# Attention and routed experts on one core: the casts of v move from GpSimd to VectorE and ScalarE

## The chip, the cores and the metric

The kernel runs on one core of a Trainium2 chip. TensorE (PE) multiplies, VectorE (DVE), ScalarE (ACT) and GpSimd (POOL) do elementwise work, and SyncE (SP) only issues transfers. SP, ACT and POOL can each issue DMA transfers, which run on the core's 16 DMA engines. Every engine works through its own queue of instructions strictly in order; an instruction that waits holds up all that stand behind it on that engine. The metric is the device time of one execution in microseconds.

## What is computed

Linear attention, then a mixture of eight experts with weights from a Sinkhorn iteration:

```python
def phi(x): return np.where(x > 0, x, np.exp(x) - 1.0) + 1.0
q_p, k_p = phi(q), phi(k)                  # q, k, v: 8 batches, 8 heads, 576 rows, 64 columns, f32
kv = np.einsum('bhsd,bhse->bhde', k_p, v)
z = np.sum(k_p, axis=2)
num = np.einsum('bhsd,bhde->bhse', q_p, kv)
den = np.einsum('bhsd,bhd->bhs', q_p, z)[..., None] + 1e-06
x = num / den                              # taken as 4608 rows of 512
P = np.exp(x @ w_gate - max)               # then eight rounds: rows and columns of P normalised
for e in range(8):
    out += P[:, e:e+1] * (np.maximum(x @ w1[e], 0.0) @ w2[e])    # w1[e]: 512x1024, w2[e]: 1024x512
```

## The kernel before

**Stages.** The front computes attention in 16 half batches, numbered n = 0 to 15 (batch n // 2, four heads each), in the function `att` (L237). Expert 0 runs beside the front in plain form (`unit_plain`, L695, with its first layer in `layer1`, L520), in nine groups of 512 rows, since its groups need only the finished rows of x. Experts 1 to 7 come after, in a form with seven block products in place of eight (`unit`, L766), whose operands are DVE sums of weight blocks (`combos`, L736). The Sinkhorn iteration (L415) needs the logits of all rows and gives the factors P by which every expert's output is scaled.

**One half batch.** Three inputs of 576 KB each (kin, qin, vin) are loaded (L253). For k and q, ACT takes the exponential (L266, tiles ek and eq, f16); DVE clamps it at 1 (L275) and takes the maximum with x + 1 (L281, two instructions; or ACT adds 1 at L272 and DVE takes one maximum at L278), giving tk and tq. v is cast from f32 to f16 into vv, beside a column of ones (L295 and L225). Two such vv buffers alternate. PE then multiplies tk by vv (kv_ps, L306), transposes tq (qt_ps, L332), forms the denominators (den_ps, L347) and the numerators in three parts (num_ps, L371). DVE takes the reciprocal (rden, L353) and multiplies (xn, L376); PE transposes xn (xt_ps, L387) and ACT or DVE copies it into xT (L221 or L223). The inputs, ek and eq together, tk, tq and most others have two buffers each, so the load for n + 2 waits for the last reader of n.

**Expert 0.** `layer1` computes hq = w1 x in eight tiles of 128 columns for each group, each a sum of four matmuls over the contraction (512 rows in four blocks c of 128; L536), and ACT applies the maximum with 0 (L540, tile h). Blocks 0 and 1 of x come from the even half batch, 2 and 3 from the odd one. hq has two PSUM buffers. The second layer (ye, L706) reads h and w2.

**Weights.** `load_w` (L192) loads and casts w1 and w2 of an expert through DMAs on POOL's queue; each kind has two buffers. For expert 0 both come in two halves. w1 of expert 0 is made to depend on the cast of v of n = 0 (`vcast[0]`, L490), w2 of expert 0 on the inputs of n = 3. Inputs of n = 2 and 3 are issued by POOL too, all others by SP.

**What sets the order.** All work is handed to `_Plan` (L18) with an engine, a duration in microseconds, dependencies and a priority. Its `run` method plays the schedule through with these durations and gives the instructions out in the order that comes of it. `LAT` and `OVER` are its figures for the hand-over between engines. What it emits is fixed: the engines later follow their queues in that order, whatever the real durations. A DMA is a task of 1.55 (an input) on one serial engine, and 2.6 until it can be used. The loads of expert 1's weights carry a start time that only the plan knows:

```python
w_t[1] = load_w1(1, prio=0.0, after=110.0) + load_w2(1, prio=0.0, after=115.0)
```

On the chip such an instruction runs when those ahead of it in POOL's queue have run and its own semaphores have come. In the built order of before, POOL's queue in the front is: v cast of n = 0, w1 of expert 0 (two DMAs), kin and qin of n = 2, v cast of n = 1, vin of n = 2, the three inputs of n = 3, w2 of expert 0 (two DMAs), w_gate, the 14 other casts of v, w1 and w2 of expert 1. 34 matmuls on a tile of zeros (L476) keep PE warm at the start. From expert 1 on, the order of PE's work is written out by hand (L885).

Of the kernel before, what the change touches and what calls it, by code (L numbers as in the profile page):

```python
# [10 lines left out]
FP32 = mybir.dt.float32  # L11
FP16 = mybir.dt.float16
# [5 lines left out]
class _Plan:  # L18
# [14 lines left out]
    def add(self, eng, fn, deps=(), prio=0.0, acq=(), use=(), lat=0.0, after=0.0):  # L33

        if isinstance(eng, tuple):
            eng = {eng[0]: eng[1]}
        k = len(self.t)
        t = {"eng": eng, "fn": fn, "prio": prio, "acq": tuple(acq), "lat": lat, "kids": [], "nd": 0,
             "ready": after, "done": None, "id": k}
        self.t.append(t)  # L40
        for d in set(x for x in deps if x is not None):
            self.t[d]["kids"].append(k)
            t["nd"] += 1
        for g in list(acq) + list(use):
            g["users"].append(k)
        return k
# [76 lines left out]
def kernel(  # L123
# [10 lines left out]
    nc = tc.nc  # L134

    B, H, S, D = q.shape
# [4 lines left out]
    P = 128  # L141
    PW = 64
    NJ = S // PW
    NG = N // 512
    NTT = N // P
    NFT = F // P
    NDT = DM // P
# [3 lines left out]
    S_ = _Plan()  # L151
    add = S_.add

    const = ctx.enter_context(tc.tile_pool(name="const", bufs=1))
# [3 lines left out]
    hqp = ctx.enter_context(tc.tile_pool(name="hqp", bufs=2, space=PSUM))  # L158
# [18 lines left out]
    fp = front.enter_context(tc.tile_pool(name="fp", bufs=2))  # L177
# [1 line left out]
    kvz_t = [fp.tile([P, 2, 2, D + 1], FP16, tag=f"kvz{i}", name=f"kvz{i}", bufs=1) for i in range(2)]  # L179

    p_in = {n: S_.pool(2) for n in "kvq"}
    p_e = S_.pool(2)
    p_t = {n: S_.pool(2) for n in "kq"}
    p_vv, p_kvz, p_qpT, p_xn, p_rden = (S_.pool(2) for _ in range(5))
    p_att, p_hq, p_h = S_.pool(2), S_.pool(2), S_.pool(2)
# [33 lines left out]
    def copy(e, dst, src):  # L219
        if e == "act":  # L220
            nc.scalar.copy(out=dst, in_=src)  # L221
        elif e == "dve":
            nc.vector.tensor_copy(out=dst, in_=src)  # L223
        else:
            nc.gpsimd.tensor_copy(out=dst, in_=src)  # L225
# [4 lines left out]
    vcast = {}  # L230

    def fadd(*a, **kw):
        t = add(*a, **kw)
        front_ids.append(t)
        return t

    def att(b, g):  # L237
        n = 2 * b + g
        pr = n - 100.0
# [7 lines left out]
        gin, tin, gt, tph = {}, {}, {}, {}  # L247
        for nm, ten in (("k", k), ("q", q), ("v", v)):
            gr = gin[nm] = S_.grp(p_in[nm])

            def fn(_, gr=gr, nm=nm, ten=ten):
# [5 lines left out]
                      deps=[w_last[0] if n in (2, 3, 4) else None, in_prev[0]])  # L257
            in_prev[0] = ti
            tin[nm] = fadd(("dma", 1.55), lambda _: None, deps=[ti], use=[gr], prio=pr, lat=2.6)
        for nm in "kq":  # L260
            ge = S_.grp(p_e)
            gt[nm] = S_.grp(p_t[nm])

            def f_e(_, ge=ge, nm=nm):
                ge["tile"] = fp.tile([P, 2, NJ, D], FP16, tag="e", name="e" + nm)
                nc.scalar.activation(out=ge["tile"], in_=gin[nm]["tile"], func=AF.Exp)  # L266

            def f_t(e, g_=gt[nm], nm=nm):
                g_["tile"] = fp.tile([P, NJ, 2, D], FP16, tag="t" + nm, name="t" + nm)
                g_["on"] = e  # L270
                if e == "act":
                    nc.scalar.add(out=g_["tile"].rearrange("p j r d -> p r j d"), in_=gin[nm]["tile"], add=1.0)  # L272

            def f_m(_, ge=ge, g_=gt[nm], nm=nm):
                nc.vector.tensor_scalar(out=ge["tile"], in0=ge["tile"], scalar1=1.0, scalar2=None, op0=ALU.min)  # L275
                o = g_["tile"].rearrange("p j r d -> p r j d")
                if g_["on"] == "act":
                    nc.vector.tensor_tensor(out=o, in0=o, in1=ge["tile"], op=ALU.max)  # L278
                else:
                    for r in range(2):  # L280
                        nc.vector.scalar_tensor_tensor(out=o[:, r], in0=gin[nm]["tile"][:, r], scalar=1.0,  # L281
                                                       in1=ge["tile"][:, r], op0=ALU.add, op1=ALU.max)
            te = fadd(("act", 1.17), f_e, deps=[tin[nm]], acq=[ge], use=[gin[nm]], prio=pr)
            tt_ = fadd({"dve": 0.6, "act": 1.17}, f_t, deps=[tin[nm]],
                       acq=[gt[nm]], use=[gin[nm]], prio=pr)
            tph[nm] = fadd(("dve", 1.35), f_m, deps=[te, tt_], use=[ge, gt[nm], gin[nm]], prio=pr)
        gvv = S_.grp(p_vv)
        tvv = []
# [3 lines left out]
        ta = fadd(("none", 0.0), f_va, deps=[tin["v"]], acq=[gvv], prio=pr)  # L292
        def f_v(e):
            copy(e, gvv["tile"][:, :, :, 0:D], gin["v"]["tile"])
        tvv.append(fadd(("pool", 1.3), f_v, deps=[ta, tin["v"]],  # L295
                        use=[gvv, gin["v"]], prio=pr))
        vcast[n] = tvv[0]
        gkv, gz = [S_.grp(p_ye[2]), S_.grp(p_ye[3])], S_.grp(p_kvz)

        def f_kv(_):  # L300
# [25 lines left out]
        for j0, j1 in ((0, 5), (5, NJ)):  # L326
# [8 lines left out]
            def f_qc(e, j0=j0, j1=j1, gp=gp):  # L335
                copy(e, gq["tile"][:, :, j0:j1, :].rearrange("p h j w -> p j h w"), gp["tile"][:, 0:j1 - j0])
            t1 = fadd(("pe", 0.06 * (j1 - j0)), f_qt, deps=[tph["q"], tqa], acq=[gp], use=[gt["q"]], prio=pr)
            tq.append(fadd({"act": 0.12 + 0.1 * (j1 - j0), "dve": 0.17 + 0.057 * (j1 - j0)}, f_qc, deps=[t1, tqa],
                           use=[gp, gq], prio=pr))
# [23 lines left out]
        for i0, i1 in ((0, 2), (2, 4), (4, 5)):  # L363
# [15 lines left out]
            t1 = fadd(("pe", 0.12 * (i1 - i0)), f_num, deps=[tden, txa], acq=[gn], use=[gq, gz], prio=pr)  # L379
            txn.append(fadd(("dve", 0.14 + 0.275 * (i1 - i0)), f_xn, deps=[t1, trd, txa], use=[gn, grd, gxn], prio=pr))  # L380
        for c2 in range(2):
# [10 lines left out]
            t1 = fadd(("pe", 0.3), f_xt, deps=txn, acq=[gx], use=[gxn], prio=pr)  # L392
# [68 lines left out]
        return add(("dve", 0.8), f_p, deps=last, prio=-200.0)  # L461

    nc.vector.memset(ones_t, 1.0)
    warm = const.tile([P, 512], FP16, tag="warm", name="warm")
    nc.vector.memset(warm, 0.0)

# [18 lines left out]
    for i in range(2):  # L485
        nc.vector.memset(vv_t[i][:, :, :, D], 1.0)
        nc.vector.memset(kvz_t[i], 0.0)
    att(0, 0)
    att(0, 1)
    w_t = {0: load_w1(0, prio=-290.0, parts=2, deps=[vcast[0]])}  # L490
    for b in range(1, B):
        att(b, 0)
        att(b, 1)
        if b == 1:
            w_t[0] += load_w2(0, prio=-96.5, parts=2, deps=[in_prev[0]])
        if b % 2 == 1:
            logits(b // 2)
# [17 lines left out]
    prev_hq = [None]  # L515
# [4 lines left out]
    def layer1(e, g):  # L520
        gw1, tw1, gw2, tw2 = w_t[e]
        bs = range(512 * g // S, (512 * g + 511) // S + 1)
        xd_ = [xt_done[(b, c)] for b in bs for c in range(NDT)]
        th = []
        gh = S_.grp(p_h)

        def f_ha(_):
            gh["tile"] = hpool.tile([P, NFT, 512], FP16, tag="h", name="h")
        tha = add(("none", 0.0), f_ha, deps=[prev_hq[0]], acq=[gh], prio=g - 400.0)
        for f in range(NFT):  # L530
            ghq = S_.grp(p_hq)

            def f_hq(_, f=f, ghq=ghq):
                ghq["tile"] = hqp.tile([P, 512], FP32, tag="hq", name="hq")
                for c in range(NDT):
                    nc.tensor.matmul(ghq["tile"], lhsT=gw1["tile"][:, c, ts(f, P)], rhs=xT[:, c, ds(512 * g, 512)],  # L536
                                     start=(c == 0), stop=(c == NDT - 1))

            def f_rl(_, f=f, ghq=ghq):
                nc.scalar.activation(out=gh["tile"][:, f, :], in_=ghq["tile"], func=AF.Relu)  # L540
            t1 = add(("pe", 0.87), f_hq, deps=[tw1[f // 4], prev_hq[0]] + xd_, acq=[ghq], use=[gw1],
                     prio=g + 0.1 * f + 0.35)
            prev_hq[0] = t1
            x_users.append(t1)
            th.append(add(("act", 0.6), f_rl, deps=[t1, tha], use=[ghq, gh], prio=g - 400.0))
        return gh, [th, th]

# [147 lines left out]
    def unit_plain(e, g, gW=None, tW=None):  # L695
        gw1, tw1, gw2, tw2 = w_t[e]
        gh, th = layer1(e, g) if e == 0 else block7(e, g, gW, tW)
        gy = [S_.grp(p_ye[tt % 2]) for tt in range(4)]
        ty = [None] * 4
# [225 lines left out]
```

The softmax here doesn't subtract the row's maximum and nothing guards it: scores larger than these inputs give would overflow.

## Time and profile before

| | us |
|---|---|
| median of 12 runs (lowest, highest) | 982.49 (981.75, 985.77) |
| the profiled execution | 982.66 |
| its span, from the first to the last instruction | 980.9 |
| PE busy | 961.2 |
| DVE busy | 770.7 |
| ACT busy | 562.9 |
| POOL busy | 128.0 |

The granted TensorE clock was 0.999 on average. The profile shows one execution. The page lists engines with their busy time; the span in 40 slices of equal length, where each digit is a busy share in tenths; and groups of instructions. Besides the page, the trace answers questions: the instructions of a stretch in order of time (start, duration, engine, line, operation, output <- inputs; in brackets, idle time before it and what ended that), sums of waiting by pair of engines (total, times, longest), and tables of busy time by stretch. PE's instructions overlap, so a row of matmuls can be shorter than the sum of their durations.

### The profile page before, as it was taken

To read this page: it belongs to the slowest core of one execution; us is meant where nothing else is said; L and a number is where in the kernel's file an instruction comes from. 1 tells how busy PE (TensorE), PEld (TensorE's weight loads), DVE (VectorE), ACT (ScalarE), POOL (GpSimd) and SP (SyncE) were. 2 spreads that over 40 slices of the span, in tenths; PEclk is the share of its full clock that TensorE was granted. 3 is DMA by queue.
4 is the path that set the end of the run, shared out by engine and by line. 5 is a ranking of instruction groups with operands and counts; after the bars stand their busy time and mean duration, and the time that the engine had idled before them with its cause. 6 is when DMAs were issued, how large, how long until landed. Compare 5 with 4: busy or idle time off the path is not lost.

```text
span 980.9 us, 21403 instructions
## 1 busy us (share of the span) xinstructions
PE 961.2 (98%) x8716; PEld 791.9 (81%) x8716; DVE 770.7 (79%) x1561; ACT 562.9 (57%) x1034; POOL 128.0 (13%) x171
## 2 busy tenths in 40 slices
PE   7899999999999999999999999999999999999997
PEld 3555564488888888888888888888888888888885
DVE  6898869967777777777777777777777777777774
ACT  4898754565555555555555555555555555555552
POOL 5111200001111111111111111111111111111110
PEclk9999999999999999999999999999999999999999
DMA  9987953162226322272226322272225322236663
GB/s 307 289 288 241 277 155 127 66 132 77 74 77 141 95 76 76 76 161 76 75 76 141 96 76 76 77 162 76 76 77 136 102 76 77 76 108 163 161 161 98
DMA packets 47028, 121.99 MB, mean 124 GB/s; under 512 B 4176, under 2 KB 18000, under 8 KB 46928
## 3 DMA queue, kind: packets, MB, share of 16 engines
q1 hardware_dynamic: 32128, 99.76, 30.8%
q0 software_dynamic: 14480, 20.33, 11.6%
q8 instruction: 68, 1.11, 0.4%
q10 hardware_dynamic: 320, 0.52, 0.1%
q14 instruction: 32, 0.26, 0.1%
HBM read 119.69 MB, written 17.69 MB: 140 GB/s over the span
## 4 chain that ended last, share of the span: by engine, by line
PE 89%; DVE 1%; ACT 1%; issue 0%
PE ye L809 33%; PE hq L627 23%; PE att L627 11%; PE Zye L627 6%; PE Zye L809 6%; PE ye L706 5%; PE hq L536 4%; PE xt_ps L387 0%; PE kv_ps L306 0%; PE num_ps L371 0%; PE lg_ps L405 0%; DVE tk L281 0%; PE qt_ps L332 0%; ACT tq L272 0%; PE den_ps L347 0%; ACT qpT L221 0%
## 5 line engine op out<-in xcount | busy, mean ns | idle before, releaser
L823 DVE SCALAR_TENSOR_TENSOR acc<-ye,P_sb,acc 128x256 f32<-128x256 f32 x620 | 264.9, 477 | 95.2 <-PE ye L809 77.8
L627 PEld LDWEIGHTS <-W 128*128 128x128 f16 x2016 | 197.0, 98 | 23.9
L809 PEld LDWEIGHTS <-S 128*128 128x128 f16 x1984 | 194.2, 98 | 22.7 <-issue 0.3
L809 PE MATMUL ye<-T,S 128*128 128x256 f16 x1488 | 192.8, 273 | 0.1
L833 POOL TENSOR_TENSOR acc<-acc,st 128x256 f32<-128x256 f32 x124 | 87.4, 725 | 625.6 <-ACT st L830 620.8
L653 ACT ACTIVATE h<-hq 128x512 f16<-128x512 f32 x126 | 76.5, 607 | 160.9 <-PE hq L627 160.9
L627 PEld LDWEIGHTS <-w 128*128 128x128 f16 x1512 | 147.5, 98 | 23.3 <-issue 1.0
L809 PEld LDWEIGHTS <-h 128*128 128x128 f16 x1488 | 145.6, 98 | 16.8
L627 PE MATMUL hq<-xs,W 128*128 128x256 f16 x1008 | 151.2, 273 | 0.0
L627 PE MATMUL att<-xs,W 128*128 128x256 f16 x1008 | 151.1, 272 | 0.0
L627 PE MATMUL hq<-xs,w 128*128 128x256 f16 x1008 | 140.7, 272 | 0.8 <-DVE h L656 0.8
L782 DVE TENSOR_TENSOR S<-h 128x1024 f16<-128x1024 f16 x124 | 85.4, 688 | 57.9 <-ACT h L653 57.9
L656 DVE CUSTOM_DVE_ANT_0 h<-att,s 128x512 f16<-128x512 f32 x126 | 86.7, 688 | 13.1 <-ACT s L643 13.1
L830 ACT ACTIVATE st<-Zye,P_sb 128x256 f32<-128x256 f32 x124 | 52.0, 470 | 78.0 <-PE Zye L809 78.0
L643 ACT COPY s<-hq 128x512 f32<-128x512 f32 x126 | 75.1, 596 | 36.8 <-PE hq L627 36.8
L650 ACT ACTIVATE h<-Zye 128x512 f16<-128x512 f32 x126 | 75.2, 597 | 35.1 <-PE Zye L627 35.1
L656 DVE CUSTOM_DVE_ANT_0 h<-hq,s 128x512 f16<-128x512 f32 x126 | 86.4, 686 | 0.8 <-PE hq L627 0.7
L639 ACT COPY Zye<-hq 128x512 f32<-128x512 f32 x126 | 73.3, 581 | 16.3 <-PE hq L627 16.3
L706 PE MATMUL ye<-w,h 128*128 128x512 f16 x320 | 77.6, 379 | 0.0
L627 PE MATMUL Zye<-xs,w 128*128 128x256 f16 x504 | 75.6, 273 | 0.0
L647 ACT COPY s<-att 128x512 f32<-128x512 f32 x126 | 74.5, 591 | 0.0
L536 PE MATMUL hq<-xT,w 128*128 128x512 f16 x288 | 70.6, 379 | 2.0 <-ACT h L540 1.7
(90 smaller groups left out, 960.3 us busy)
## 6 DMA issues: line engine op xcount, KB each, us to landing
xs<-xd SPq DMA_DIRECT2D x63, 896.0 KB, 4.6
w<-in_moe_w_dram POOLq DMA_DIRECT2D x14, 1024.0 KB, 11.3
out_dram<-acc SPq DMA_DIRECT2D x68, 128.0 KB, 2.4
kin<-in_k_dram SPq DMA_DIRECT2D x14, 576.0 KB, 6.1
qin<-in_q_dram SPq DMA_DIRECT2D x14, 576.0 KB, 5.5
vin<-in_v_dram SPq DMA_DIRECT2D x14, 576.0 KB, 6.6
xd<-xst SPq DMA_DIRECT2D x9, 512.0 KB, 2.6
xd<-xT SPq DMA_DIRECT2D x9, 256.0 KB, 5.0
```

Source lines behind the costliest of these rows:

```text
L536: nc.tensor.matmul(ghq["tile"], lhsT=gw1["tile"][:, c, ts(f, P)], rhs=xT[:, c, ds(512 * g, 512)], start=(c == 0), stop=(c == NDT - 1))
L627: nc.tensor.matmul(dst[:, p, :], lhsT=lhs(p, c), rhs=rhs(c), start=(first and p == 0 and c == 0), stop=(c == 1), skip_group_check=True)
L643: nc.scalar.copy(out=gs2["tile"], in_=gX["tile"])
L647: nc.scalar.copy(out=gs5["tile"], in_=gR["tile"])
L650: nc.scalar.activation(out=hd(0, 0), in_=Zt[1], func=AF.Relu)
L653: nc.scalar.activation(out=hd(1, 0), in_=gX["tile"], func=AF.Relu)
L656: nc.vector._custom_dve(TENSOR_ADD_SAT, out=dst, in0=ps, in1=sb, s0=3.0e38, s1=0.0)
L706: nc.tensor.matmul(gy[tt]["tile"], lhsT=gh["tile"][:, f, ds(P * tt, P)], rhs=gw2["tile"][:, f, :], start=(f == 0), stop=(f == NFT - 1))
L782: nc.vector.tensor_tensor(out=Sx[:, i], in0=a0, in1=a1, op=op)
L809: nc.tensor.matmul(bank(g_)[:, s, :], lhsT=lhs(s, kk), rhs=rhs(kk), start=(new and s == 0 and kk == 0), stop=(kk == 3), skip_group_check=True)
L823: nc.vector.scalar_tensor_tensor(out=dst(), in0=bank(g_)[:, s, :], scalar=P_sb[:, gg, e:e + 1], in1=dst(), op0=ALU.mult, op1=ALU.add)
L833: nc.gpsimd.tensor_tensor(out=dst(), in0=dst(), in1=gst["tile"], op=ALU.add)
```

## The change

v is cast by ACT for n = 0 and 1 and by DVE for n = 2 to 15. POOL copies four columns of v of n = 0 into a small tile `gate`, and w1 of expert 0 depends on that copy. ek and eq share three buffers, not two. In the first group of expert 0, the first two tiles of hq are computed in halves of the contraction: each product over blocks 0 and 1 is a step of its own that needs only the even half batch.

```diff
--- before.py
+++ after.py
@@ -179,7 +179,7 @@
     kvz_t = [fp.tile([P, 2, 2, D + 1], FP16, tag=f"kvz{i}", name=f"kvz{i}", bufs=1) for i in range(2)]
 
     p_in = {n: S_.pool(2) for n in "kvq"}
-    p_e = S_.pool(2)
+    p_e = S_.pool(3)
     p_t = {n: S_.pool(2) for n in "kq"}
     p_vv, p_kvz, p_qpT, p_xn, p_rden = (S_.pool(2) for _ in range(5))
     p_att, p_hq, p_h = S_.pool(2), S_.pool(2), S_.pool(2)
@@ -262,7 +262,7 @@
             gt[nm] = S_.grp(p_t[nm])
 
             def f_e(_, ge=ge, nm=nm):
-                ge["tile"] = fp.tile([P, 2, NJ, D], FP16, tag="e", name="e" + nm)
+                ge["tile"] = fp.tile([P, 2, NJ, D], FP16, tag="e", name="e" + nm, bufs=3)
                 nc.scalar.activation(out=ge["tile"], in_=gin[nm]["tile"], func=AF.Exp)
 
             def f_t(e, g_=gt[nm], nm=nm):
@@ -292,9 +292,12 @@
         ta = fadd(("none", 0.0), f_va, deps=[tin["v"]], acq=[gvv], prio=pr)
         def f_v(e):
             copy(e, gvv["tile"][:, :, :, 0:D], gin["v"]["tile"])
-        tvv.append(fadd(("pool", 1.3), f_v, deps=[ta, tin["v"]],
+        tvv.append(fadd(("act", 1.17) if n < 2 else ("dve", 0.75), f_v, deps=[ta, tin["v"]],
                         use=[gvv, gin["v"]], prio=pr))
-        vcast[n] = tvv[0]
+        if n == 0:
+            def f_gate(_):
+                nc.gpsimd.tensor_copy(out=gate, in_=gin["v"]["tile"][:, 0, 0, 0:4])
+            vcast[0] = add(("pool", 0.15), f_gate, deps=[tin["v"]], use=[gin["v"]], prio=pr)
         gkv, gz = [S_.grp(p_ye[2]), S_.grp(p_ye[3])], S_.grp(p_kvz)
 
         def f_kv(_):
@@ -461,6 +464,7 @@
         return add(("dve", 0.8), f_p, deps=last, prio=-200.0)
 
     nc.vector.memset(ones_t, 1.0)
+    gate = const.tile([P, 4], FP32, tag="gate", name="gate")
     warm = const.tile([P, 512], FP16, tag="warm", name="warm")
     nc.vector.memset(warm, 0.0)
 
@@ -527,21 +531,29 @@
         def f_ha(_):
             gh["tile"] = hpool.tile([P, NFT, 512], FP16, tag="h", name="h")
         tha = add(("none", 0.0), f_ha, deps=[prev_hq[0]], acq=[gh], prio=g - 400.0)
-        for f in range(NFT):
-            ghq = S_.grp(p_hq)
-
-            def f_hq(_, f=f, ghq=ghq):
-                ghq["tile"] = hqp.tile([P, 512], FP32, tag="hq", name="hq")
-                for c in range(NDT):
+        ghqs = [S_.grp(p_hq) for f in range(NFT)]
+        jobs = [(f, 0, NDT) for f in range(NFT)]
+        if g == 0:
+            jobs = [(f, c, c + 2) for c in (0, 2) for f in range(2)] + jobs[2:]
+        for f, c0, c1 in jobs:
+            ghq = ghqs[f]
+
+            def f_hq(_, f=f, ghq=ghq, c0=c0, c1=c1):
+                if c0 == 0:
+                    ghq["tile"] = hqp.tile([P, 512], FP32, tag="hq", name="hq")
+                for c in range(c0, c1):
                     nc.tensor.matmul(ghq["tile"], lhsT=gw1["tile"][:, c, ts(f, P)], rhs=xT[:, c, ds(512 * g, 512)],
                                      start=(c == 0), stop=(c == NDT - 1))
 
             def f_rl(_, f=f, ghq=ghq):
                 nc.scalar.activation(out=gh["tile"][:, f, :], in_=ghq["tile"], func=AF.Relu)
-            t1 = add(("pe", 0.87), f_hq, deps=[tw1[f // 4], prev_hq[0]] + xd_, acq=[ghq], use=[gw1],
+            t1 = add(("pe", 0.2175 * (c1 - c0)), f_hq, deps=[tw1[f // 4], prev_hq[0]] + xd_[0:c1 if g == 0 else None],
+                     acq=[ghq] if c0 == 0 else [], use=[gw1] + ([ghq] if c0 > 0 else []),
                      prio=g + 0.1 * f + 0.35)
             prev_hq[0] = t1
             x_users.append(t1)
+            if c1 < NDT:
+                continue
             th.append(add(("act", 0.6), f_rl, deps=[t1, tha], use=[ghq, gh], prio=g - 400.0))
         return gh, [th, th]
```

In the built order of the changed kernel, POOL's queue in the front is: the gate copy, w1 of expert 0 (two DMAs), the six inputs of n = 2 and 3, w2 of expert 0 (two DMAs), w_gate, w1 and w2 of expert 1, and then the same as before. w1 and w2 of expert 1 wait there for the landing of qin and of vin of n = 2. DVE has 14 instructions more than before, ACT two more, POOL 15 fewer. On ACT the cast of n = 0 stands between eq of n = 0 and ek of n = 1, that of n = 1 behind the addition for tq of n = 1. Other work that may run on either engine is spread anew: four copies of xT, among them both of n = 1, go from ACT to DVE. On DVE the first xn of n = 4 stands behind the work for tk of n = 7. On PE one early half product stands ahead of den_ps of n = 1, the other behind xt_ps of n = 1; from the first matmul of expert 1 on, PE's order is the same.

## The prediction

> **What bounds the kernel now.** First the page's head and slices, to find the engine and the stage.
>
> ```profile
> PE 961.2 (98%) x8716; PEld 791.9 (81%) x8716; DVE 770.7 (79%) x1561; ACT 562.9 (57%) x1034; POOL 128.0 (13%) x171
> ...
> PE   7899999999999999999999999999999999999997
> ...
> DMA  9987953162226322272226322272225322236663
> ```
>
> PE is full but for the first four slices and the last. Then the stretches I cut from that: PE busy 13.83 of 20.00, 7.32 of 10.00 and so on.
>
> ```profile
> 0.00:20.00 20.00, 13.83 (x129) 7.36 (x130) 13.56 (x31) 9.46 (x13) 11.46 (x19) 1.00 0.96 288
> 20.00:30.00 10.00, 7.32 (x67) 3.70 (x65) 7.16 (x16) 6.58 (x10) 2.73 (x3) 1.00 1.11 318
> ...
> 57.40:130.00 72.60, 68.42 (x728) 42.08 (x727) 63.02 (x135) 59.59 (x95) 12.73 (x11) 1.00 0.85 257
> 130.00:900.00 770.00, 769.92 (x6840) 658.95 (x6838) 609.11 (x1227) 426.63 (x806) 89.51 (x125) 1.00 0.34 98
> ```
>
> The columns are PE, PEld, DVE, ACT, POOL, granted clock, share of the DMA engines, GB/s. From 130 to 900 us PE lacks 0.08 us, and the change leaves the matmuls there in the same order. So the time is PE's work plus PE's gaps in the first 130 us. Those are 6.2 up to 20 us, 2.7 up to 30, and 4.2 in 57.4 to 130. The DMA engines are full (1.11) just there. PE's waits over the first 130 us:
>
> ```profile
> PE xt_ps L387 <- DVE xn L376: 3.2, 5, 1.2
> PE kv_ps L306 <- POOL vv L225: 2.6, 1, 2.6
> PE hq L536 <- ACT h L540: 1.7, 2, 1.4
> PE qt_ps L332 <- DVE tq L281: 1.4, 2, 0.8
> ```
>
> Last the timeline, where the same pair of DVE instructions costs 2.25 beside a Pool cast and 1.43 without one:
>
> ```profile
> 8.11 1.47 POOL L225 CAST vv<-vin 128x1152 f16<-128x1152 f32 x1 [6.80 <-DMA vin<-in_v_dram]
> ...
> 109.81 1.41 POOL L225 CAST vv<-vin 128x1152 f16<-128x1152 f32 x1 [4.17 <-DMA vin<-in_v_dram]
> 111.17 1.62 POOL L207 DMA_DIRECT2D w<-in_moe_w_dram  x2
> ```
> ```profile
> 8.61 2.25 DVE L281 SCALAR_TENSOR_TENSOR tq<-qin,eq 128x576 f16<-128x576 f32 x2
> ...
> 25.25 1.43 DVE L281 SCALAR_TENSOR_TENSOR tk<-kin,ek 128x576 f16<-128x576 f32 x2
> ```
>
> The last POOL line matters most: expert 1's weights have no wait of their own that would hold them back. They leave at 111.17 only because they stand behind the 16th cast in Pool's queue. I write n0 to n15 for the half batches.
>
> **Step 1, the start: 2.4 us gained by 31 us.** v of n0 lands at 8.11. ACT's cast, by the exp of the same tile 1.16, ends at 9.27, Pool's at 9.58, so kv_ps starts 0.3 earlier. The DVE instruction beside the Pool cast falls from 1.58 to 0.76, and one at 12.97 from 1.70 to 0.76. So DVE is at xn of n0 at 13.9 and not 15.18, and everything of n1 moves by 1.3. Its xT copies go from ACT (ended 23.49) to DVE: done at 21.9. ACT no longer has them ahead of ek of n2, which therefore starts when k lands (19.49, where the wg_sb issue was released) and not at 23.38. The early contraction halves take places where warm matmuls stood; they cost nothing and give at most the 0.43 of two matmuls. Before, den_ps of n2 started at 30.81 behind five hq groups. Now six groups stand ahead, and ACT, DVE and PE add up to 29.3. Gain: 1.5 + 0.87 = 2.4. The third exp buffer and the halves are inside this sum. What is late next is w2's second half: its wait stands at 38.80 before, would be reached at 36.5, and k, q, v of n4 now leave about 3 us sooner and share the engines with it. It costs 0 to 2.7, and step 3 swallows it.
>
> **Step 2, DVE trades contention for casts: 2.0 us gained later.** Summed over its instructions beside the 16 casts, DVE loses 6.2 us (worst 0.8 to 0.94, some nothing). It gets 14 casts instead. No row shows a DVE cast of 128x1152 from f32. Below stands the clamp of 1152 f16 elements, 0.45; above, two instructions over 576 f32 elements each, 1.51. I take 0.76, the DVE maximum over 1152 elements (L278), nearest in size: 10.6 us in all, DVE +4.4. DVE is busy 63.02 of 72.60 in 57.4 to 130, and the built order answers by placing attention later: kv_ps of n15 stands behind 108.6 us of PE work, 102.0 before. (PE's work is counted by start-to-start distances: 0.865 for four matmuls of 512 columns, 0.62 for kv_ps, 0.56 for ten xt_ps, and so on.) So DVE mostly keeps its lead. The stretched instructions (58.39, 63.54, 69.71, 75.06) sit where PE has its gaps of 0.97 and 1.74. Of the 4.2 us of gaps I take away half: 2.0, bounds 0 and 4.2.
>
> [...]
>
> **Step 3, expert 1's weights leave 88 us sooner: 6.7 us lost.** In the built order Pool's queue is gate copy, w1, six inputs, w2, w_gate, and then at once both weight matrices of expert 1. They wait only for the landing of q and v of n2 (v: 23.75). So they follow w_gate on the DMA engines, around 36 to 38 us, while inputs are due. The price of the transfer: the rate per microsecond is 175 to 210 GB/s while weights are written and about 400 for inputs, so 1 MB of weights takes 5.0 and one input of 590 kB 1.48. From 26.2, where w2 begins, to the landing of k of n7 the engines owe w2 5.0, w_gate 0.7, expert 1 10.0, and ten inputs 14.8: 30.5, so 56.7, and 58.0 with 1.3 from last byte to landing. Before, k of n7 was issued at 47.47 and took 5.1: 52.6. Bounds: 51.6 if it is issued 1 us sooner and the weights yield wholly; 60 if it also meets the stragglers that gave q of n7 6.7.
>
> Who waits: on DVE xn of n4 stands behind tk of n7, which needs exp 1.16, clamp 0.46 and two additions 1.43; the first xn takes 0.69. So 58.0 + 3.7 = 61.7. On PE the third num_ps group of n4 waits for that xn, with xt_ps, kv_ps of n6 and all else queued behind. It stands behind 42.4 us of PE work. Before, PE had done as much at 57.4; with step 1 it would be there at 55.0. So PE idles 6.7 us, against before it is 4.3 later; 2.1 earlier at the lower bound, 6.3 later at the upper. ACT's queue waits at the same exp, relus behind it.
>
> [...]
>
> **Step 4, the handover: 0.4 lost.** The last logits stand 5.2 us of PE work later, so the Sinkhorn steps and the 32 scalings do too. DVE had 1.71 us idle at 194.00; the built order lets two of expert 1's h pass ahead of the remaining scalings. PE's only wait beyond 130 is 0.8 (hq on DVE h); I add half of that. Bounds 0 and 2. The weights' old place (111 to 128) becomes free: worth nothing, PE lacks nothing from 120 on.
>
> **The sum.** Step 1 is contained in step 3's 4.3. 4.3 - 2.0 + 0.4 = +2.7 on the profiled execution's 982.66 (span 980.9 and 1.8 around it): **985.4**, own range 984.6 to 988. The profiled execution lies 0.17 above the median of 12, far less than the steps' uncertainty.
>
> **Rivals.**
> - *A wash, 0.28.* The weights take less than their half of the engines, k of n7 lands at 55: 4.3 becomes 1.3 and the sum -0.3, 982.4. For it: inputs have gaps (share 0.72 in 40 to 50 us) that weights can fill.
> - *Faster, 0.25.* The weights cost nothing: k of n7 at 51.6 or n4's xn not held by it. -2.1 - 2.0 + 0.4 = -3.7: 979.0. For it: step 1 and the lost contention are well shown by rows. Against: 10 us more of transfers between 26 and 57, where the engines lacked only some 4.
> - *Slower by another way, 0.09.* DVE's cast costs 1.51. From ek of n7 on DVE's rows add up to 74 us for about 70 of PE's; nine casts at 0.75 more make it 81, DVE becomes the bound, PE waits some 5 more: 990.
> - *The gate doesn't gate:* it holds only expert 0's w1; for expert 1 nothing replaces the casts. That is the forecast, 0.38.
>
> **How the numbers follow.** A run of this kernel can tell about 0.2% (2 us) from no change. Slower: 0.38 + 0.09 = 0.47. Within: 0.28. Faster: 0.25. Range: down to the faster case's 979.0, up past the forecast's upper bound for k of n7 (+6.3 - 2.0 + 0.4, 987.4) to 989.
>
> **What would show it.** Step 1: den_ps of n2 near 29.3. Step 2: L281 at 0.76 throughout, casts near 0.76. Step 3: Pool's two weight issues near 22 to 24 us instead of 111; k of n7 landing near 58; PE waiting some 5 us in 54 to 62, released by DVE xn. It is wrong if PE runs through 50 to 62 without a gap, or if casts on DVE take over 1.2.

## The result and the profile after

The changed kernel took 985.44 us (median of 12 runs, 984.74 to 986.25); the kernel before took 982.25 (48 runs). The ratio is 1.0028, 95% interval [1.0021, 1.0036]: 0.28% slower. The profiled execution took 986.25 us with a span of 984.5, 3.6 more than before's 980.9.

The head and the slices of the page of the changed kernel:

```profile
PE 963.0 (98%) x8716; PEld 791.9 (80%) x8716; DVE 773.3 (79%) x1575; ACT 564.9 (57%) x1036; POOL 110.4 (11%) x156
...
PE   7789999999999999999999999999999999999997
...
DMA  9986725262225322272225422272225322236663
```

PE runs the same 8716 matmuls, but is busy 1.8 us longer, and its idle time (span less busy) is 21.5 us, 19.7 before. So half of the loss is idle time and half is matmuls that took longer. The loss arises early: expert 1's first matmul starts at 197.22 us, at 193.80 before, which is 3.4 of the 3.6 us. The stretches, in the columns of before:

```profile
0.00:20.00 20.00, 15.17 (x140) 8.08 (x141) 13.54 (x35) 11.65 (x14) 8.39 (x18) 1.00 0.97 296
20.00:30.00 10.00, 8.59 (x77) 4.55 (x75) 9.17 (x19) 7.99 (x15) 2.23 (x3) 1.00 1.09 336
57.40:130.00 72.60, 70.38 (x729) 42.29 (x728) 65.14 (x144) 63.14 (x103) 0.00 (x0) 1.00 0.72 244
130.00:900.00 770.00, 769.87 (x6876) 658.76 (x6875) 610.42 (x1232) 425.92 (x805) 91.32 (x124) 1.00 0.34 97
```

Three of four stretches are better or the same: PE does 1.3 us more by 20 us and 1.3 more from 20 to 30, and its gaps from 57.4 to 130 are 2.2 us where they were 4.2. What these lines leave out is the stretch between. From 31 to 60 us, in the kernel before:

```profile
31.00:60.00 29.00, 28.13 (x326) 17.36 (x323) 25.19 (x54) 24.68 (x44) 4.61 (x4) 1.00 0.89 288
```

and in the changed kernel:

```profile
31.00:60.00 29.00, 21.22 (x208) 11.54 (x203) 18.07 (x38) 18.19 (x30) 0.00 (x0) 0.94 1.12 305
```

PE lost 6.9 us here, at a mean clock of 0.94, with the DMA engines full (1.12, before 0.89). PE's waits over the first 130 us of the changed kernel (total, times, longest):

```profile
PE hq L545 <- ACT h L549: 3.7, 3, 2.0
PE ye L718 <- DMA w<-in_moe_w_dram: 3.6, 2, 2.7
PE kv_ps L309 <- ACT vv L221: 2.5, 1, 2.5
PE yw L480 <- DVE warm L469: 1.3, 1, 1.3
PE num_ps L374 <- DVE xn L379: 1.1, 3, 0.5
```

The second line is new: PE stands before ye because expert 0's w2 hasn't landed. The wait for the cast of v is still there (2.5, before 2.6), now on ACT. The timeline of POOL and DVE shows what the change did to their queues:

```profile
8.19 0.19 POOL L299 COPY gate<-vin 128x4 f32<-128x4 f32 x1 [6.88 <-DMA vin<-in_v_dram]
...
22.35 0.74 POOL L207 DMA_DIRECT2D w<-in_moe_w_dram  x1 [1.74 <-DMA qin<-in_q_dram]
23.85 0.88 POOL L207 DMA_DIRECT2D w<-in_moe_w_dram  x1 [0.77 <-DMA vin<-in_v_dram]
```
```profile
24.02 1.43 DVE L281 SCALAR_TENSOR_TENSOR tq<-qin,eq 128x576 f16<-128x576 f32 x2
25.36 0.76 DVE L223 CAST vv<-vin 128x1152 f16<-128x1152 f32 x1
```

Expert 1's weights leave at 22.35 and 23.85 us instead of 111. The pair at L281 takes 1.43 now, and a cast 0.76. Last the chain that ended last, from 18 to 54 us:

```profile
18.34 21.05 DMA w<-in_moe_w_dram
...
45.77 1.12 ACT ek L266
46.89 6.90 DMA kin<-in_k_dram
...
53.81 0.90 ACT ek L266
```

Read it from the bottom. ACT's exp of half batch 6 starts at 53.81, when its k lands. That k was issued at 46.89 (42.18 before) and took 6.90 us to land (4.28 before). Above it stands the landing of w2's second half at 39.39.

### The profile page after: what moved, and what is told of

It reads as the page before. It is cut to its first block, busy times and chain, and to the rows that moved or that the text cites. A ratio compares the mean times of both kernels' runs of the same rounds, so it can differ in the third digit from the quotient of the medians.

```text
span 984.5 us, 21392 instructions
## 1 busy us (share of the span) xinstructions
PE 963.0 (98%) x8716; PEld 791.9 (80%) x8716; DVE 773.3 (79%) x1575; ACT 564.9 (57%) x1036; POOL 110.4 (11%) x156
## 4 chain that ended last, share of the span: by engine, by line
PE 89%; DMA 5%; DVE 3%; ACT 2%; issue 1%; DVEq 0%; ACTq 0%
PE ye L821 33%; PE hq L639 23%; PE att L639 11%; PE Zye L639 6%; PE Zye L821 6%; PE ye L718 5%; PE hq L545 4%; DMA w<-in_moe_w_dram 3%; DMA kin<-in_k_dram 1%; DMA qin<-in_q_dram 1%; PE num_ps L374 1%; DVE tq L281 0%; ACT h L549 0%; DVE xn L379 0%; ACT ek L266 0%
## 5 line engine op out<-in xcount | busy, mean ns | idle before, releaser
L718 PE MATMUL ye<-w,h 128*128 128x512 f16 x320 | 79.6, 384 | 4.2 <-DMA w<-in_moe_w_dram 3.6
```

The lines of the kernel that those rows point to most:

```text
L718: nc.tensor.matmul(gy[tt]["tile"], lhsT=gh["tile"][:, f, ds(P * tt, P)], rhs=gw2["tile"][:, f, :], start=(f == 0), stop=(f == NFT - 1))
```

## The experiments

My theory after this trace had three terms: expert 1's weights among the inputs, the earlier wait for w2, and the slow clock behind that wait. The rivals: the price is the casts on DVE; or only one of the three terms counts. Every run was timed against the kernel before on the same chip. Hold, early, w2first and hold_w2 shared one chip, the next four after them in the table another, hold_nohalf, hold_ek and after_ek a third, hold_plan a fourth; across these groups the ratios compare better than the medians. "k of 6 lands" is when the last of the 16 engines ended that transfer, by the trace of the profiled execution.

| kernel | median us | ratio to before [95%] | k of 6 lands | PE busy, idle in its profile |
|---|---|---|---|---|
| before | 982.25 | | 46.5 | 961.2, 19.7 |
| changed | 985.44 | 1.0028 [1.0021, 1.0036] | 53.8 | 963.0, 21.5 |
| hold | 982.61 | 1.0003 [0.9994, 1.0012] | 49.3 | 963.4, 18.7 |
| early | 988.47 | 1.0065 [1.0052, 1.0077] | 54.0 | 964.9, 21.6 |
| w2first | 990.67 | 1.0087 [1.0074, 1.0101] | 52.2 | 965.3, 23.3 |
| hold_w2 | 986.63 | 1.0051 [1.0038, 1.0063] | 46.1 | 967.1, 16.9 |
| after_warm | 985.60 | 1.0035 [1.0022, 1.0047] | 53.5 | 964.0, 20.4 |
| hold_warm | 982.91 | 1.0009 [1.0000, 1.0018] | 49.3 | 965.3, 15.6 |
| poolcast | 985.11 | 1.0035 [1.0022, 1.0049] | 44.4 | 961.6, 20.0 |
| hold_2e | 984.58 | 1.0026 [1.0015, 1.0037] | 51.0 | 963.1, 20.8 |
| hold_nohalf | 983.12 | 1.0009 [1.0000, 1.0017] | 49.1 | 963.4, 17.4 |
| hold_ek | 986.05 | 1.0035 [1.0023, 1.0047] | 50.3 | 966.8, 20.2 |
| after_ek | 990.62 | 1.0084 [1.0070, 1.0098] | 53.1 | 968.7, 20.7 |
| hold_plan | 983.76 | 1.0016 [1.0007, 1.0025] | 44.2 | 962.6, 19.4 |

### hold: expert 1's weights held back again

```diff
+        if n == 15:
+            def f_hold(_):
+                nc.gpsimd.tensor_copy(out=gate, in_=gin["v"]["tile"][:, 0, 0, 0:4])
+            vcast[15] = add(("pool", 0.15), f_hold, deps=[tin["v"]], use=[gin["v"]], prio=pr)
...
-    w_t[1] = load_w1(1, prio=0.0, after=110.0) + load_w2(1, prio=0.0, after=115.0)
+    w_t[1] = load_w1(1, prio=0.0, after=110.0, deps=[vcast[15]]) + load_w2(1, prio=0.0, after=115.0, deps=[vcast[15]])
```

> The changed kernel, except that expert 1's two weight tiles leave only behind a small Pool copy of the v of half batch 15 (near 110-125 us, about where they left before the change) instead of at 22 us. TensorE's order is the same as in the changed kernel. Theory (part of the loss is these 2 MB among the inputs of half batches 5 to 7): the k of half batch 6 lands 3 to 5 us sooner than 53.8 and the k of 7 sooner than 59.0, TensorE's waits on ACT's relus at 56.7 and 59.8 shrink, the 2.65 us wait for the second half of w2 and the clock's drop at 39-44 us stay; 982.3 to 983.5. Rival 1 (the early wait for w2 and the clock are all of it, the transfers cost nothing): 985 to 985.6, with w2's wait unchanged. Rival 2 (the casts on VectorE are the price): 985.4, and the expert blocks no different.

982.61 us: 2.8 below the changed kernel, and level with the kernel before. (Its profiled execution took 983.86, 1.25 above the median.) PE's waits from 31 to 60 us in its trace:

```profile
PE ye L722 <- DMA w<-in_moe_w_dram: 2.3, 1, 2.3
PE qt_ps L339 <- DVE xT L223: 1.1, 1, 1.1
PE ye L722 <- ACT h L553: 0.6, 1, 0.6
PE hq L549 <- ACT h L553: 0.5, 1, 0.5
```

The k of 6 landed at 49.3, 4.5 us sooner. The wait on ACT's relus in this stretch fell from 2.0 to 0.5; of the two for w2 the longer stayed (2.3, it was 2.7). The theory's numbers held, and both rivals are out: the casts on DVE were still there. So in this order of the work the early weights cost 2.8 us (2.5 by the ratios).

### early: the weights' early start alone, in the kernel before

```diff
+        for nm, ten, ap in (("w1", moe_w1, [[F, P], [F * P, NDT], [1, F]]), ("w2", moe_w2, [[DM, P], [DM * P, NFT], [1, DM]])):
+            w_early[nm] = wpool.tile([P, ap[1][1], ap[2][1]], FP16, tag=nm, name=nm)
+            nc.gpsimd.dma_start(out=w_early[nm], in_=AP(tensor=ten.tensor, offset=DM * F, ap=ap))
```

These lines stand behind the load of w_gate; at its old place the load only takes over these tiles.

> The kernel before, with expert 1's two weight tiles issued right behind the gate weights on Pool's queue and nothing else altered: casts on Pool, two exp buffers, TensorE's order the same. Theory (the early weights alone cost 2 to 4 us, by later inputs of half batches 5 to 7): 984 to 986.3, with the k of 6 and of 7 landing 3 to 6 us later than 46.5 and 52.6. Rival (there is slack for them in the kernel before; only the changed order has none): 982 to 983. Pool's casts of half batches 2 and 3 start up to 3 us later for the two issues, which may add up to 1 us.

988.47 us, 0.65% above the kernel before, more than the theory allowed. The k of 6 landed at 54.0, as in the changed kernel. But the experiment carries a second cost: the cast of v of n2 stands behind the two new issues on POOL's queue and starts 1.1 us later (24.82, before 23.75). DVE is later too, and one pair of its instructions now meets the next cast (2.37 us at 28.17, before 1.43). PE's waits over the first 130 us:

```profile
PE kv_ps L308 <- POOL vv L226: 3.1, 2, 1.7
PE qt_ps L334 <- DVE tq L283: 2.7, 2, 2.1
```

The 2.1 for tq, at 28.5 us, belongs to that second cost. The second wait for vv (1.4, ended at 54.30) does not: it is for the v of 5, which landed at 52.56, before at 42.61, so it is part of what the weights themselves cost. The two costs aren't separated here; the run shows the direction and the landing of k, not the price.

### w2first and hold_w2: w2 ahead of the inputs of half batch 3

```diff
+        if b == 1:
+            w_t[0] += load_w2(0, prio=-97.5, parts=2, deps=[in_prev[0]])
         att(b, 1)
-        if b == 1:
-            w_t[0] += load_w2(0, prio=-96.5, parts=2, deps=[in_prev[0]])
```

> The changed kernel, except that Pool issues expert 0's w2 before the inputs of half batch 3 instead of behind them; the schedule planned around it moves a little too. Theory (TensorE reaches w2 before it has landed, and the idle makes the clock drop): the two waits of 0.99 and 2.65 us at 33.8 and 39.4 go, the granted clock stays at 1.00 up to 50 us, and of the 3.6 us of waits and the 1.5 us of slow clock 2.5 to 4.5 us come back, the rest being taken by the later inputs of half batch 3: 981 to 983. Rival 1 (the weights of expert 1 among the inputs are all of it): the same later inputs of 6 and 7 bind at 54-60 us whatever comes before, 985 to 986. Rival 2 (the casts): 985.4.

> The changed kernel with both edits of the two runs above: expert 1's weights leave behind the v of half batch 15, and expert 0's w2 leaves before the inputs of half batch 3. If both terms are real and separate, the sum is 2 to 3 us and 2.5 to 4.5 us below 985.4: 978 to 981, faster than the kernel before by 1 to 4 us, since the start's gain and the quieter VectorE then stay. If they are the same idle counted twice: 981 to 983. If VectorE's casts are the price: 985.

Both expectations failed: 990.67 and 986.63 us. The wait for w2 is gone in both, and others take its place. PE's two longest waits from 31 to 60 us in w2first:

```profile
PE xt_ps L390 <- ACT xT L221: 4.6, 1, 4.6
PE den_ps L350 <- ACT qpT L221: 1.8, 1, 1.8
```

And its stretches of 2 us there (the last three columns are clock, DMA share and GB/s):

```profile
44.00:46.00 2.00, 1.06 (x12) 0.81 (x13) 1.90 (x5) 1.09 (x2) 0.00 (x0) 1.00 1.13 290
46.00:48.00 2.00, 0.00 (x0) 0.00 (x0) 0.81 (x2) 1.59 (x4) 0.00 (x0) 0.52 1.13 292
...
56.00:58.00 2.00, 2.00 (x27) 1.61 (x25) 1.51 (x4) 0.87 (x2) 0.00 (x0) 0.50 1.04 403
58.00:60.00 2.00, 2.00 (x8) 0.78 (x7) 1.68 (x3) 1.79 (x5) 0.00 (x0) 0.57 1.06 399
```

The clock stayed at half from 46.1 to 59.7 us, over both waits and more than 5 us of full work behind them. The k of 6 was issued at 40.87 and landed at 52.2, 11.36 us later: the early issue didn't help behind the weights. Holding them back brought the landing to 46.1 and the time down by 4.0. That is a second measurement of their price, in another order of the work; a third, after_ek against hold_ek below, gives 4.6. So the price depends on the order around the weights.

### after_warm and hold_warm: does the slow clock cost anything?

```diff
+                    if (e, g, tt, half) == (0, 0, 0, 1):
+                        for _i in range(8):
+                            nc.tensor.matmul(gy[0]["tile"], lhsT=warm[:, 0:P], rhs=warm, start=False, stop=False)
```

hold_warm also has eight matmuls into the warm-up bank ahead of the first kv product.

> The changed kernel with only the eight zero matmuls ahead of the first product with the second half of w2. Theory: the clock's drop at 39 to 43 us goes, and with it up to 1.5 us: 983.9 to 984.6. Rival (behind it TensorE waits for the k of half batches 6 and 7 in any case, which expert 1's weights hold up): nothing is gained, 985.2 to 985.8, and the waits at 47.7 and 54.7 us grow by what the clock gave back.

> The held-back version (expert 1's weights behind the v of half batch 15, 982.6 us) with two fillers for TensorE: eight 128x512 matmuls into the warm-up bank ahead of the first kv product, and eight that add zeros ahead of the first product with the second half of w2. They lie in waits of 2.5 to 3.0 and of 2.3 us and leave the result as it is. Theory (after those waits the clock runs at half speed for some 3 us and takes 1.5 to 2 us each time it does): the clock stays at 1.00 from 6 to 50 us, TensorE's busy time up to the expert blocks falls from 181.9 towards 180 us plus 3.4 us of fillers, and the time is 980 to 981.5. Rival (the slow clock only eats work that would have waited for transfers anyway): 982.3 to 983.

In the changed kernel the clock stayed at 1.00 from 36 to 44 us with the fillers, and the wait for w2 fell from 3.6 to 1.6. The time didn't move: 985.60. The waits of after_warm from 31 to 60 us:

```profile
PE hq L545 <- ACT h L549: 3.5, 1, 3.5
PE ye L721 <- DMA w<-in_moe_w_dram: 1.6, 2, 0.9
```

The 2.0 of the changed kernel has become 3.5: PE reaches the relus sooner, and they still stand behind the exp of a k that lands at 53.5. Behind that longer wait the clock fell again (0.50 in 56 to 58). The rival was right: the slow clock at 39 to 43 us used time that would have been lost waiting. For the changed kernel my term for the clock falls. In hold_warm the median is 982.91, 0.3 above hold, with overlapping intervals; the spread is narrower (982.24 to 983.33, where hold had 980.84 to 984.58). In hold the drop isn't quite free, though. In its profiled execution the clock fell to half at 38.2 us, behind the wait for w2; in those of hold_warm and hold_nohalf it didn't, and there the den_ps near 110 us start 0.6 us sooner (109.79 and 109.81, in hold 110.37). What the fillers themselves cost isn't measured.

### poolcast: v's cast back on POOL from half batch 2

```diff
-        tvv.append(fadd(("act", 1.17) if n < 2 else ("dve", 0.75), f_v, deps=[ta, tin["v"]],
+        tvv.append(fadd(("act", 1.17) if n < 2 else ("pool", 1.3), f_v, deps=[ta, tin["v"]],
```

> The changed kernel with v's cast back on Pool from half batch 2 on, all else as in the change (first two casts on ACT, the gate, three exp buffers, first products by halves). Expert 1's weights are then held back by Pool's casts, as before the change. Theory (the casts on VectorE are worth some 2 us by ending the stretched VectorE instructions, the early weights cost some 3): 983.5 to 985.5, that is 1 to 3 us above the held-back version's 982.6, with gaps of 3.5 to 4.5 us on TensorE from 57 to 130 us. Rival 1 (the casts' place is worth nothing, only the weights count): 982 to 983. Rival 2 (the cast on VectorE is itself a cost): below 982.

985.11 us (983.40 to 987.83), 2.5 above hold, as the theory had it. Its stretch from 57.4 to 130 us:

```profile
57.40:130.00 72.60, 68.39 (x725) 41.75 (x724) 59.79 (x128) 58.81 (x94) 10.85 (x10) 1.00 0.77 235
```

PE lacks 4.2 us, exactly as in the kernel before; with the casts on DVE it lacks 2.2. DVE's instructions are stretched again too: the pair for tk at 60.12, beside a cast on POOL at 60.70, takes 2.38, where the changed kernel has 1.43 throughout. So the casts' place is worth 2.0 us of gaps, and a DVE that does more work leaves PE less idle. The profiled execution took 983.4, the lowest of the five; what lengthens the others isn't shown by a trace.

### hold_2e and hold_nohalf: the other two parts of the change

```diff
-    p_e = S_.pool(3)
+    p_e = S_.pool(2)
...
-                ge["tile"] = fp.tile([P, 2, NJ, D], FP16, tag="e", name="e" + nm, bufs=3)
+                ge["tile"] = fp.tile([P, 2, NJ, D], FP16, tag="e", name="e" + nm, bufs=2)
```
```diff
-            jobs = [(f, c, c + 2) for c in (0, 2) for f in range(2)] + jobs[2:]
+            jobs = [(f, 0, NDT) for f in range(2)] + jobs[2:]
```

> The held-back version with two exp buffers in place of three. Theory (the third buffer lets ACT take the next k while VectorE still clamps the last, which is worth little since VectorE and the transfers set the pace): 982.6 to 983.8. Rival (the third buffer is what pulls the inputs of half batch 4 ahead of w2 and so makes the wait at 35 us): w2's wait falls below 1 us and the clock does not drop there: 979.5 to 981.5.

> The held-back version with expert 0's first two products of group 0 whole again instead of by contraction halves. Theory (the halves are worth under half a us: the products wait for the same xT and end before w2 has landed in any case): 982.3 to 983.2. Rival (they fill TensorE's gaps at 22 to 28 us and save that time): 983.5 to 984.5. Rival 2 (they bring TensorE to w2 too early): 981 to 982.

With two exp buffers the time is 984.58, 2.0 above hold and above both expectations. The w2 wait grew, against the rival. PE's gaps are 0.9 us longer from 31 to 45 us and 1.0 from 57.4 to 130, and the k of 6 lands 1.6 later. So the third buffer is worth about 2 us. Without the halves it is 983.12, 0.5 above hold with overlapping intervals: they are worth nothing that these runs can tell. The first two casts on ACT and the gate were not taken away by themselves.

### hold_ek, after_ek and hold_plan: where did the start's gain go?

hold has the faster start and the quieter DVE, and yet only the old time. Its k of 6 is issued at 45.42, 3.2 us later than before's. I first held ACT responsible:

```diff
-            te = fadd(("act", 1.17), f_e, deps=[tin[nm]], acq=[ge], use=[gin[nm]], prio=pr)
+            te = ek_t[n, nm] = fadd(("act", 1.17), f_e, deps=[tin[nm]], acq=[ge], use=[gin[nm]], prio=pr)
...
-                tf = add({"act": 0.59, "dve": 0.69}, f_fin, deps=[ty[tt], t_close if g >= NA else None],
+                tf = add({"act": 0.59, "dve": 0.69}, f_fin, deps=[ty[tt], t_close if g >= NA else None, ek_t[4, "k"] if g == 0 and tt == 0 else None],
```

> The held-back version, with one dependency more in the plan: the first eviction of expert 0's second product (acc from ye) comes behind ACT's exp of the k of half batch 4 in ACT's order instead of ahead of it. Found in the traces: in the changed and in the held-back kernel ACT stands idle from 36.2 to 39.7 us before that eviction, which waits for w2, with the k of 4 landed since 31 us behind it; so the buffer of that k comes free 4 to 5 us later, and the k of 6 is issued at 45.4 to 46.9 us where the kernel before had 42.2. Theory (this is where the start's gain went): the k of 6 is issued near 41.5 us and lands near 45, the waits on ACT's relus between 45 and 60 us go, 979 to 981, the first version faster than the kernel before. Rival (transfers set the pace up to 60 us in any order): 982 to 983, with the k of 6 still landing after 48 us.

> The changed kernel with only that dependency: the exp of the k of half batch 4 ahead of the first acc eviction in ACT's order, expert 1's weights leaving early as in the change. If the late issue of the k of 6 and the early weights are separate costs: 982 to 983.5, 2 to 3.5 us below the changed kernel, the weights' 3 us left. If the weights' transfers bind the inputs of 6 and 7 whatever their issue time: 984.8 to 985.6.

In hold_ek the exp moved to 36.2 us as intended, and the k of 6 was still issued at 46.00 and landed at 50.3: the theory about ACT fell. The times, 986.05 and 990.62, are above all that was expected. The plan, given the new dependency, also placed later work otherwise, and both traces show a new loss there: a wait of 1.8 us for xn (from 70.8 us in hold_ek, 73.5 in after_ek), and behind it the clock at half for 6.8 us. Whether that is all of the excess isn't shown. The timeline of DVE in the changed kernel shows what really held the k of 4:

```profile
36.82 0.42 DVE L223 COPY qpT<-qt_ps 128x512 f16<-128x512 f16 x1 [0.91 <-PE qt_ps L335]
41.58 0.18 DVE L356 TENSOR_SCALAR rden<-den_ps 128x20 f32<-128x20 f32 x1 [4.34 <-PE den_ps L350]
...
45.39 1.43 DVE L281 SCALAR_TENSOR_TENSOR tk<-kin,ek 128x576 f16<-128x576 f32 x2
```

DVE stood idle 4.34 us in front of rden, which waits for den_ps, which stands behind ye on PE, which waits for w2. The instruction that reads the k of 4 last (tk at L281) is queued behind it and ends at 46.82; the next k is issued at 46.89. The last experiment corrects the order at its root, the plan's belief about which transfer lands first:

```diff
-            tin[nm] = fadd(("dma", 1.55), lambda _: None, deps=[ti], use=[gr], prio=pr, lat=2.6)
+            tin[nm] = fadd(("dma", 1.55), lambda _: None, deps=[ti], use=[gr], prio=pr - (1.0 if n == 4 else 0.0), lat=2.6)
```

> The held-back version, with the plan's model of the transfers put right at one place: the inputs of half batch 4 are taken to be served ahead of expert 0's w2, as the traces show it (k of 4 landed at 30.6 to 31.5 us, second half of w2 at 37.9 to 39.4; the plan had them the other way round, 35.3 and 34.5). No DMA is moved on its queue by it; what moves is the order of VectorE, ACT and TensorE. The kernels so far leave VectorE idle from 37 to 40 us, in front of a rden that waits through TensorE for w2, with the clamp of the k of 4 queued behind it; that clamp, done at 45.3 us, is what frees the buffer, and putting ACT's exp ahead alone did not move it (issue of the k of 6 at 46.0 us). Theory (the start's gain is lost in that clamp): the clamp runs by 38 us, the k of 6 is issued by 39 and lands by 44 us, TensorE's waits between 35 and 60 us fall from 4.5 towards 2 us: 978.5 to 981, and below the kernel before. Rival (the transfers set TensorE's pace to 60 us in any order of the engines): 982 to 983.5.

tk ran at 35.00, the k of 6 was issued at 36.50 and landed at 44.2, 2.3 us sooner than in the kernel before. And yet 983.76 us, just past the rival's end. PE's wait for w2 is gone, and this one from 31 to 60 us is new:

```profile
PE den_ps L354 <- ACT xT L221: 2.8, 1, 2.8
```

ACT's xT stands there behind the exp of the q of 4, which started at 35.06; the q landed at 34.98, and DVE's clamp of ek, which the trace names as the releaser, ended in the same moment. Behind this wait the clock was at half for nearly 7 us:

```profile
36.00:38.00 2.00, 0.15 (x6) 0.15 (x6) 1.82 (x4) 1.80 (x3) 0.00 (x0) 0.50 1.18 348
38.00:40.00 2.00, 2.00 (x18) 1.10 (x16) 1.73 (x5) 0.00 (x0) 0.00 (x0) 0.50 1.07 395
40.00:42.00 2.00, 2.00 (x9) 0.88 (x7) 0.69 (x1) 0.00 (x0) 0.00 (x0) 0.50 1.06 407
```

Over the whole profile PE is idle 0.3 us less than in the kernel before and busy 1.4 us more. So the slow clock is a rival here to the wait itself, and no run with fillers separates them. In each of three orders (hold, hold_w2, hold_plan) PE had a gap of 1.2 to 2.8 us between 35 and 48 us, before another engine or transfer each time. In none did the start's gain survive to 60 us. Whether some order keeps it isn't settled. No version's median beat the kernel before.

## Why the prediction was right, and where it was not

The predicted 985.4 is the measured 985.44, and the sign's cause was the one named. But the sum hides two errors that cancel, by luck: the weights were put 3.9 us too dear (6.7 for 2.8), and hold, the change without them, took 982.61 where the working's other terms give some 979.

**Step 1, the start: right in size.** den_ps of n2 started at 28.76 (predicted 29.3), and PE's gaps up to 31 us fell from 8.85 to 6.24, 2.6 us (predicted 2.4). The working had the third exp buffer and the halves inside this sum, but they are hardly in it: den_ps of n2 still started at 28.95 with two buffers and at 28.91 without the halves. The 2.0 us that the buffer is worth arise later.

**"It costs 0 to 2.7, and step 3 swallows it": this is the sentence that failed.** The wait for w2's second half came as sized: 2.65 us, reached at 36.8 (predicted 36.5); one of 0.99 for the first half was not foreseen. But step 3 doesn't swallow it. In hold, without the early weights, the start's gain is gone all the same. The wait also keeps the last reader of the k of 4 from running, some 4 us of idle DVE, so the next k is issued 3 to 5 us later than before. I had let k, q, v of later half batches leave sooner because the start was faster.

**Step 2, DVE: right.** The casts on DVE took 0.70 to 0.77 (0.76 assumed), L281 1.43 a pair throughout, and the gaps from 57.4 to 130 us fell by 2.0, as predicted; poolcast gives the 2.0 back.

**Step 3, the weights: right in kind, wrong in size and place.** They were issued at 22.35 and 23.85 and landed at 47.8 and 55.4. The k of 7 landed at 59.0 (predicted 58.0). The wait came one half batch earlier than I put it: ACT waited 1.53 us for the k of 6, and PE for the relus behind it (2.0 us, ended at 56.70, where I had some 5 released by xn on DVE). At the third num_ps of n4, where I had put 6.7 us of idle, PE waited 0.38 for xn, at 63.9 us. The term itself is 2.8 us (changed against hold), where the working had 6.7 of idle. The total came out right because the start's gain was lost by another way, which I hadn't priced. The 1.3 us from last byte to landing in the working is shown by no run: for the v of 5 in the kernel before, the last packet ended at 42.19 and the landing stands at 42.61, 0.42 us later.

**Step 4, the handover: nothing.** From 130 to 900 us PE lacks 0.13 us, before 0.08. The 0.4 wasn't there.

**The rivals.** The wash assumed that the weights take less than their half of the transfers (15.7 of the 30.5 us in the working) and that k of 7 lands at 55; it landed at 59.0. The faster case had the weights cost nothing; they cost 2.8. Had they cost nothing, the time would have been hold's 982.61, not 979.0. DVE's cast wasn't dear (0.76, where that rival had 1.51). "The gate doesn't gate" was right: no instruction of the change holds expert 1's weights.

## What to carry to other kernels

When work leaves an in-order queue, list what stood behind it: a transfer that only waited its turn now starts as soon as the queue is free and its own semaphores have come, whatever start time a planner had for it (here expert 1's w1 at 22.35 us, at 111.17 before, with 110.0 in the plan). A gain ahead of a stretch that is bound by transfers isn't a gain until that stretch has been worked through with the new order; ask which instruction frees each input buffer, and behind which wait it is queued. A total that comes out right proves none of its terms; take each away by itself.

## What was not expected of the hardware

The granted clock of TensorE fell to half around these short waits. In the changed kernel, at the end of a wait of 2.65 us:

```profile
36.00:38.00 2.00, 0.78 (x11) 0.54 (x9) 0.42 (x1) 0.69 (x1) 0.00 (x0) 1.00 1.18 325
38.00:40.00 2.00, 0.57 (x2) 0.25 (x2) 0.00 (x0) 0.00 (x0) 0.00 (x0) 0.83 1.15 302
40.00:42.00 2.00, 2.00 (x16) 0.87 (x14) 0.38 (x2) 0.66 (x2) 0.00 (x0) 0.50 1.10 274
42.00:44.00 2.00, 2.00 (x14) 1.05 (x13) 0.97 (x3) 2.00 (x3) 0.00 (x0) 0.82 1.10 271
```

Four ye matmuls took 1.86 us there, and 1.03 elsewhere. A wait of 2.56 us at 7.1 us in the kernel before was followed by no drop; one of 1.72 at 7.7 us in hold_w2 was (0.57 in 10 to 12 us). So the length of one wait doesn't decide it.

What fits is the share of a window in which PE was busy. By the traces' record of the clock, the stretches at half last 3.41 us or a multiple of it (39.31 to 42.72 us in the changed kernel, 35.62 to 42.45 in hold_plan, 46.09 to 59.74 in w2first). I read the first 130 us of all 14 traces in windows of that length, in step with these stretches. All 16 windows at full clock in which PE was busy for 48% or less were followed by half clock; of the 475 busier ones only two were (53% in hold_plan, 57% in w2first). The window ahead of the drop above was 26% busy, that in hold_w2 45%; the two at the wait in the kernel before were 54% and 53%. This was read from the traces afterwards, not tested.

No run leaves out the 34 zero matmuls of the start, so what they do for the clock isn't shown. With eight more ahead of the first kv product (hold_warm) the clock was 1.00 from 6 to 16 us, where hold had 0.61 from 10 to 14.
